# Head mixing for two groups at once on four 64x64 tiles of TensorE

## The chip, the core and the metric

The kernel runs on one core of a Trainium2 chip. The metric is the device time of one execution in microseconds. A core has a matrix engine (TensorE, PE in the profile, with PEld for its weight loads), a vector engine (VectorE, DVE), a scalar engine (ScalarE, ACT), a general engine (GpSimd, POOL) and a queue engine (SyncE, SP). The engines run side by side and wait for one another by semaphores; each works through its own instructions in the order in which the program issues them. TensorE writes to PSUM, a memory of eight banks, from which VectorE and ScalarE copy results to SBUF.

## The reference

Attention whose heads are mixed before and after the softmax, then a mixer over tokens and channels:

```python
batch, n_heads, seq, head_dim = (4, 12, 448, 64)

scores = scale * np.matmul(q, k.transpose(0, 1, 3, 2))
scores = np.einsum('bhij,hg->bgij', scores, w_pre)
scores = scores - np.max(scores, axis=-1, keepdims=True)
attn = np.exp(scores)
attn = attn / (np.sum(attn, axis=-1, keepdims=True) + 1e-09)
attn = np.einsum('bhij,hg->bgij', attn, w_post)
out = np.matmul(attn, v)          # [batch, head, seq, 64] -> x [batch, seq, 768]

xt = x.transpose(0, 2, 1)
h = np.maximum(xt @ w_tok1, 0.0) @ w_tok2      # 448 -> 256 -> 448
u = x + h.transpose(0, 2, 1)
h2 = np.maximum(u @ w_ch1, 0.0) @ w_ch2        # 768 -> 1536 -> 768
return u + h2
```

All of it is float32, and the head mixing (12x12) is what the change is about.

## The kernel before

**Row blocks and groups.** The 448 query rows of a batch are cut into four row blocks of 120, 120, 120 and 88 (`IT`); the 16 row blocks of all batches are numbered T. A row block is cut into *groups* of ten rows (`GR`), so it has 12 groups, or 9 in the last of a batch (eight of ten rows, one of eight). There are 180 groups in all, numbered G; `first[T]` is the first group of row block T. In a group, 10 rows x 12 heads = 120 pairs (row, head) lie on the partitions, with 448 key positions behind each. So one matmul with a 120x120 block matrix (`kpre`: `w_pre` repeated for each row) mixes the heads of ten rows.

**A group's way.** `qk` computes the scores of one head pair of a row block and evicts them from PSUM to the tile `s`, one head by ScalarE and one by VectorE; six such *score steps* make a row block. For T < 2 both heads sit in the two halves of the partitions and each matmul uses 64 rows of the array in float32; for T >= 2 queries are split into a rounded part and a remainder (type float32r), and a score step is four matmuls. `regroup` gathers a group's 120 rows by a DMA on the SP queue into a tile `r`. `pre` is the mixing matmul into a PSUM bank; `mx` takes the row maximum (VectorE); `ex` the exponential with its row sum (ScalarE); `rec` adds 1e-9, takes the reciprocal (VectorE) and scales the post-mixing matrix by it (GpSimd, tile `wr`). `post` is four matmuls with pieces of the exponential as stationary operand and `wr` as moving one, so it mixes heads, normalizes and transposes at once; `hi` (ScalarE) copies its PSUM bank to the tile `at`. After each two row blocks `end_av` issues a burst of `av` matmuls (attention times values, two heads on two column halves of the array), whose results go to DRAM. After the attention come the token mixer and the channel mixer, which the change does not touch.

**Splitting.** `conv_k` rounds one K head into a float32r tile and computes the remainder on GpSimd; `conv_q` does the same for half of a row block's queries. The rounding copy is VectorE's. `load_k`, `load_q` and `load_v` are their DMAs, on SP.

**Order of the work.** The order of issue is written out by hand. The main loop runs over G. In an iteration stand: `regroup` for groups ahead (up to 8 tiles `r`), loads that are due, `pre(G + 3)` (`AH = 3`), `rec(G + 2)`, `mx` and `ex` of G + 3, the score steps due (`qk_at`), an `av` burst at the start of every second row block, `post(G)`, `hi(G)`, and the splits due (`do`). The tables `qk_at` and `do` are filled before the loop: with `f = first[T - 1]`, the six score steps of row block T stand at groups f - 7 + h*n//6 with n = `first[T] - f - 3`; the splits of the next batch's K heads go two to a group.

PSUM has eight banks: two for `av`, two for `qk`, two for `pre`, two for `post`.

## Time and profile before

| | |
|---|---|
| time, median of 3 runs | 917.74 us (916.89 to 918.32) |
| the profiled execution | 916.27 us |
| its span, first to last instruction | 914.5 us |
| TensorE busy | 884.7 us |
| granted TensorE clock, mean | 0.998 |
| first and last `pre` start | 17.4 and 462.0 us |
| first and last `post` start | 22.8 and 467.3 us |
| first matmul of the channel mixer | 560.0 us |

The profile is one execution as the hardware recorded it. A row of its groups names the line of the kernel, the engine, the operation, output <- inputs, shapes and count, then the busy time in us and the mean ns of one, then the idle time of that engine just before these instructions with what ended it. A timeline row has start (us), length (us), engine, line, operation and count; consecutive instructions of a line are merged. A bracket at its end is the engine's idle time before it, with what ended it. A float32 matmul stands as two MATMUL records, a float32r matmul as one. Records of matmuls overlap, so the distance between starts, not the length, tells what one costs in a stream.

### The profile page before, as it was taken

How to read it: one execution, taken by the hardware profiler on the slowest of the kernel's cores; microseconds unless marked ns; L12 is line 12 of the kernel's file. 1: busy time of each engine (PE TensorE's matmuls, PEld its weight loads, DVE VectorE, ACT ScalarE, POOL GpSimd, SP SyncE). 2: the span in 40 equal slices, each digit the busy share in tenths (PEclk: the TensorE clock that was granted, in tenths of full speed). 3: DMA queues.
4: the chain of work that ended last, by engine and by line, in shares of the span. 5: the costliest groups of instructions: out<-in, count | busy, mean ns of one | idle time of the engine just before them, and what ended most of it. 6: DMA issues, size and time to landing. Idle time of an engine off the chain costs nothing.

```text
span 914.5 us, 14650 instructions
## 1 busy us (share of the span) xinstructions
PE 884.7 (97%) x5107; PEld 723.8 (79%) x5107; DVE 470.3 (51%) x1083; ACT 395.1 (43%) x941; POOL 321.8 (35%) x345
## 2 busy tenths in 40 slices
PE   8799899998999989999989999999999999999998
PEld 3467677776777767777767888999999999999997
DVE  3755664657646576463468999998310120031002
ACT  3366575665656557665675453443200100010000
POOL 1764743447434474341355567774000000000000
PEclk9999999999999999999999999999999999999999
DMA  5845445744457444542555666554400030000001
GB/s 167 196 144 153 113 137 134 200 144 119 137 141 193 146 118 137 142 151 94 128 188 157 202 231 192 174 165 146 177 0 1 1 121 1 1 27 34 0 1 61
DMA packets 75689, 109.16 MB, mean 119 GB/s; under 512 B 27729, under 2 KB 62048, under 8 KB 75104
## 3 DMA queue, kind: packets, MB, share of 16 engines
q1 hardware_dynamic: 68272, 101.64, 38.0%
q10 hardware_dynamic: 7312, 6.57, 2.3%
q8 instruction: 41, 0.67, 0.3%
q14 instruction: 32, 0.26, 0.1%
q0 software_dynamic: 32, 0.02, 0.0%
HBM read 53.15 MB, written 16.52 MB: 76 GB/s over the span
## 4 chain that ended last, share of the span: by engine, by line
PE 83%; DVE 6%; POOL 3%; issue 3%; ACT 2%; DMA 1%; SPq 1%; ACTq 0%; POOLq 0%; DVEq 0%
PE post L237 13%; PE pre L201 11%; PE av L254 7%; PE qk L181 7%; PE pc L514 6%; PE pc L515 6%; PE pc L513 6%; PE po L515 6%; PE po L514 6%; PE po L513 6%; PE pt L513 2%; PE pt L514 2%; PE pt L515 2%; ACT e L214 2%; DVE sm L207 2%
## 5 line engine op out<-in xcount | busy, mean ns | idle before, releaser
L237 PEld LDWEIGHTS post<-wr,e 120*112 120x112 f32 (+1 forms) x1440 | 172.7, 177 | 61.0 <-issue 36.4
L237 PE MATMUL post<-wr,e 120*112 120x120 f32 (+1 forms) x1440 | 179.8, 268 | 12.6 <-POOL wr L226 11.3
L201 PE MATMUL pre<-r,kpre 120*120 120x448 f32 x360 | 167.2, 547 | 5.0 <-ACT e L214 4.8
L214 ACT ACTIVATE e<-pre,sm 120x448 f32<-120x448 f32 x180 | 114.2, 634 | 129.8 <-DVE sm L207 129.2
L226 POOL TENSOR_SCALAR wr<-kpost,sm 120x120 f32<-120x120 f32 x180 | 110.4, 615 | 169.9 <-DVE sm L224 117.4
L207 DVE TENSOR_REDUCE sm<-pre 120x1 f32<-120x448 f32 x180 | 112.2, 623 | 103.2 <-PE pre L201 98.4
L510 DVE SCALAR_TENSOR_TENSOR rl<-pc,rh 128x448 fp32r<-128x448 f32 x48 | 29.9, 622 | 221.5 <-ACT rh L509 221.5
L509 ACT ACTIVATE rh<-pc 128x448 fp32r<-128x448 f32 x48 | 26.1, 543 | 238.2 <-PE pc L515 238.2
L181 PE MATMUL qk<-k,qc 128*120 128x448 f32 (+1 forms) x336 | 111.6, 453 | 0.2 <-ACT s L182 0.2
L514 PE MATMUL pc<-u,w 128*128 128x448 f32 x288 | 105.2, 365 | 0.0
L513 PE MATMUL pc<-u,w 128*128 128x448 f32 x288 | 105.2, 365 | 0.0
L515 PE MATMUL pc<-u,w 128*128 128x448 f32 x288 | 105.2, 365 | 0.0
L515 PE MATMUL po<-rh,w 128*128 128x448 f32 x288 | 105.2, 365 | 0.0
L513 PE MATMUL po<-rh,w 128*128 128x448 f32 x288 | 105.2, 365 | 0.0
L514 PE MATMUL po<-rl,w 128*128 128x448 f32 x288 | 105.2, 365 | 0.0
L243 ACT COPY at<-post 112x480 f32<-112x480 f32 x180 | 102.9, 571 | 5.2 <-PE post L237 5.0
L370 POOL TENSOR_SCALAR cv_g<-cv_g 128x384 f32<-128x384 f32 (+2 forms) x56 | 87.1, 1555 | 20.2 <-ACT cv_g L364 20.2
L181 PEld LDWEIGHTS qk<-k,qc 128*120 128x120 f32 (+1 forms) x336 | 58.2, 175 | 40.1 <-issue 26.9
L254 PE MATMUL av<-at,v 112*64 112x240 f32 (+1 forms) x768 | 74.6, 354 | 0.6 <-ACT x L265 0.6
L254 PEld LDWEIGHTS av<-at,v 112*64 112x64 f32 x768 | 54.4, 137 | 20.2 <-issue 1.5
L182 DVE COPY s<-qk 120x448 f32<-120x448 f32 (+1 forms) x96 | 59.7, 622 | 14.4 <-PE qk L176 8.2
L153 POOL TENSOR_TENSOR qc<-rq,qc 128x720 fp32r<-128x720 f32 (+1 forms) x28 | 46.6, 1663 | 40.7 <-DVE qc L152 32.1
(70 smaller groups left out, 1185.6 us busy)
## 6 DMA issues: line engine op xcount, KB each, us to landing
r<-s SPq DMA_DIRECT2D x176, 210.0 KB
cv_r<-in_w_ch_dram SPq DMA_DIRECT2D x48, 384.0 KB
rq<-in_q_dram SPq DMA_DIRECT2D x40, 180.0 KB
xr<-x_dr SPq DMA_DIRECT2D x8, 672.0 KB
u_dr<-u SPq DMA_DIRECT2D x24, 224.0 KB
ur<-u_dr SPq DMA_DIRECT2D x4, 1344.0 KB
out_dram<-ur SPq DMA_DIRECT2D x24, 224.0 KB
rk<-in_k_dram SPq DMA_DIRECT2D x18, 224.0 KB
```

The costliest lines, as they stand in the source:

```text
L181: nc.tensor.matmul(out=p[s][:n, :S], lhsT=l[:, g % 6, :], rhs=kt, start=i == 0, stop=i == 1)
L201: nc.tensor.matmul(out=p[:m, :S], lhsT=kpre[:m, :m], rhs=R.pop(G)[:m], start=True, stop=True)
L207: nc.vector.tensor_reduce(out=s[:m, 0:1], in_=PP[G][:m, :S], axis=AX.X, op=ALU.max, negate=True)
L214: nc.scalar.activation(out=e[:m], in_=PP.pop(G)[:m, :S], func=ACTF.Exp, bias=s[:m, 0:1], scale=1.0, accum_out=s[:m, 1:2])
L226: nc.gpsimd.tensor_scalar(out=w[:m, :m], in0=(kpost if n == GR else kpost8)[:m, :m], scalar1=s[:m, 3:4], scalar2=None, op0=ALU.mult)
L237: nc.tensor.matmul(out=p[:JP, j * m:(j + 1) * m], lhsT=l, rhs=w[:m, :m], start=True, stop=True)
L243: nc.scalar.copy(out=AT[:, :, :, o:o + IT[t][1]][:, :, :, rows(G)[1]], in_=PO.pop(G)[:JP, :JT * H * n].rearrange("p (j g i) -> p j g i", j ...
L254: nc.tensor.matmul(out=p[64 * s:64 * s + 64, :N], lhsT=V[:, 2 * hp + s, j, :], rhs=AT[:, j, 2 * hp + s, :N], start=j == 0, stop=j == JT - 1,)
L370: nc.gpsimd.tensor_scalar(out=g[:P], in0=g[:P], scalar1=MAG_MIN, scalar2=MAG_MAX, op0=ALU.max, op1=ALU.min,)
L513: nc.tensor.matmul(out=p, lhsT=a[0], rhs=x[0], start=first, stop=False)
L514: nc.tensor.matmul(out=p, lhsT=a[0], rhs=x[1], start=False, stop=False)
L515: nc.tensor.matmul(out=p, lhsT=a[1], rhs=x[0], start=False, stop=last)
```

## The change

Groups are worked on in pairs of neighbours (`steps`: pairs within a row block, the group of eight rows alone). The main loop runs over steps.

- `pre` for a pair: the 120 rows of each group's tile `r` now stand at partitions 4 to 123, so that five query rows lie in each half of 64 partitions. Four matmuls of 64 (or 60) rows by 64 columns use the four quarters of the array: array rows x take half x of both tiles, array columns s take group s. The bank of the pair's first group gets the first five query rows of both groups, the other bank the last five of both. `kpre` becomes one 60-column block in each half of the partitions; a group of eight rows uses its own matrix `kpre8` on the whole array.
- Tiles behind it have 128 partitions with four unused rows in each half; `kpost` has zeros there. `hi` writes two runs of five columns for each (key piece, head), where it wrote one of ten.
- `AH` is 2 steps (four groups). `pre` has four PSUM banks; `qk` uses the two banks of `av` (or two of `pre` in half of the first score steps).
- For T > 1 both score evictions are VectorE's. The rounding copies of `conv_k` and `conv_q` are ScalarE's.
- The splits of K heads go one to a group; the first row block's query split is two groups later, some K loads two or three groups earlier.
- At the start: three more small DMAs and ten memsets on GpSimd, and a few more operations for the constants.

The diff at its core:

```diff
-AH = 3
+AH = 2
...
-    kcat = mid.tile([120, 34], F32, bufs=1, name="kcat")
-    kpre = mid.tile([120, 120], F32, bufs=1, name="kpre")
-    kpost = mid.tile([120, 120], F32, bufs=1, name="kpost")
+    kcat = [mid.tile([128, 34], F32, bufs=1, name=f"kcat{i}") for i in range(2)]
+    kpre = mid.tile([128, 64], F32, bufs=1, name="kpre")
+    kpost = mid.tile([128, 120], F32, bufs=1, name="kpost")
+    kpre8 = mid.tile([96, 96], F32, bufs=1, name="kpre8")
     kpost8 = mid.tile([96, 96], F32, bufs=1, name="kpost8")
+    rt = [mid.tile([128, S], F32, bufs=1, name=f"r{i}") for i in range(NR)]
...
-        nc.vector.tensor_copy(out=t[p:p + 64], in_=r)
+        nc.scalar.copy(out=t[p:p + 64], in_=r)
...
-        nc.vector.tensor_copy(out=t[0], in_=r)
+        nc.scalar.copy(out=t[0], in_=r)
...
-            p = [ps.tile([128, 512], F32, tag=w, name="qk") for w in ("pre", "post")]
+            p = [ps.tile([128, 512], F32, tag="pre", bufs=4, name="qk") for s in range(2)]
         else:
-            p = [ps.tile([128, 512], F32, tag="qk", name="qk") for s in range(2)]
+            p = [ps_av.tile([128, 512], F32, tag="av", name="qk") for s in range(2)]
...
-            (nc.vector.tensor_copy if s else nc.scalar.copy)(out=S_t[T][:n, g, :], in_=p[s][:n, :S])
+            (nc.vector.tensor_copy if s or T > 1 else nc.scalar.copy)(out=S_t[T][:n, g, :], in_=p[s][:n, :S])
...
-        r = mid.tile([120, S], F32, tag="r", bufs=NR, name="r")
-        nc.sync.dma_start(out=r[:12 * n], in_=rows(G)[0](S_t[4 * b + t], 0))
-        R[G] = r
-
-    def pre(G):
-        m = 12 * groups[G][3]
-        p = ps.tile([128, 512], F32, tag="pre", name="pre")
-        nc.tensor.matmul(out=p[:m, :S], lhsT=kpre[:m, :m], rhs=R.pop(G)[:m], start=True, stop=True)
-        PP[G] = p
+        o = 4 if n == GR else 0
+        nc.sync.dma_start(out=rt[G % NR][o:o + 12 * n], in_=rows(G)(S_t[4 * b + t], 0))
+
+    def pre(st):
+        for g in st:
+            PP[g] = ps.tile([128, 512], F32, tag="pre", bufs=4, name="pre")
+        if len(st) == 1:
+            G = st[0]
+            nc.tensor.matmul(out=PP[G][:96, :S], lhsT=kpre8, rhs=rt[G % NR][:96], start=True, stop=True)
+            return
+        for x, g in enumerate(st):
+            k = slice(64 * x, 64 + 60 * x)
+            for s, a in enumerate(st):
+                nc.tensor.matmul(
+                    out=PP[g][64 * s:64 * s + 64, :S], lhsT=kpre[k], rhs=rt[a % NR][k], start=True, stop=True
+                )
+
+    def parts(G):
+        return 128 if groups[G][3] == GR else 96
...
-            out=w[:m, :m], in0=(kpost if n == GR else kpost8)[:m, :m], scalar1=s[:m, 3:4], scalar2=None, op0=ALU.mult
+            out=w[:m, :12 * n], in0=kpost if n == GR else kpost8, scalar1=s[:m, 3:4], scalar2=None, op0=ALU.mult
...
+            l = e[:k, JP * j:JP * j + JP]
+            nc.tensor.matmul(out=p[:JP, j * m:(j + 1) * m], lhsT=l, rhs=w[:k, :m], start=True, stop=True)
...
-        nc.scalar.copy(
-            out=AT[:, :, :, o:o + IT[t][1]][:, :, :, rows(G)[1]],
-            in_=PO.pop(G)[:JP, :JT * H * n].rearrange("p (j g i) -> p j g i", j=JT, g=H),
-        )
+        d = AT.rearrange("p j g i -> p (j g) i")
+        p = PO.pop(G)[:JP, :JT * H * n]
+        if n < GR:
+            d, p = d[:, :, o + 10:o + 88:11], p.rearrange("p (q i) -> p q i", i=n)
+        else:
+            w = 10 if t < 3 else 11
+            a = o + w * (c - c % 2)
+            d = d[:, :, a:a + 2 * w].rearrange("p q (s i) -> p q s i", s=2)[:, :, :, 5 * (c % 2):5 * (c % 2) + 5]
+            p = p.rearrange("p (q s i) -> p q s i", s=2, i=5)
+        nc.scalar.copy(out=d, in_=p)
...
-    nc.gpsimd.dma_start(out=kcat, in_=wcat)
+    for i in range(2):
+        nc.gpsimd.memset(kcat[i], 0.0)
+    nc.gpsimd.dma_start(out=kcat[0][4:124], in_=wcat)
+    for s in range(2):
+        nc.gpsimd.dma_start(out=kcat[1][64 * s:64 * s + 60], in_=wcat[60 * s:60 * s + 60])
+    nc.gpsimd.dma_start(out=kpre8[:, :34], in_=wcat[:96])
+    for r in rt:
+        nc.gpsimd.memset(r[:4], 0.0)
...
+    steps = []
+    G = 0
+    while G < NG:
+        n = 2 if groups[G][2] % 2 == 0 and groups[G][3] == GR else 1
+        steps.append(list(range(G, G + n)))
+        G += n
+    for st in steps[:AH]:
+        pre(st)
+        for g in st:
+            mx(g)
+            ex(g)
+    for g in steps[0]:
+        rec(g)
+    qk(1, 2)
+    pre_done = steps[AH][0]
...
-    for h in range(H):
-        at(h // 2, conv_k, 0, h)
+    for i, g in enumerate((0, 0, 1, 1, 2, 5, 6, 7, 8, 9, 9, 10)):
+        at(g, conv_k, 0, i)
     for T in range(2, NT):
         f = first[T - 1]
-        n = f if T == 1 else first[T] - f - 3
+        n = first[T] - f - 4
         for h in range(HP):
             g = f - LR + 3 + h * n // HP
             qk_at.setdefault(g, []).append((T, h))
             if T % 4 == 3 and T + 1 < NT:
-                c = [f - LR + 7 + max(0, 3 * i // 2) for i in (h, h - KB)]
-                at(c[1] + 2 if h >= KB else f - LR - 2 + h, load_k, T // 4 + 1, h)
-                for s in range(2):
-                    at(c[0] + s, conv_k, T // 4 + 1, 2 * h + s)
+                c = [f - 6 + i + 2 * (i > 6) for i in range(H)]
+                at(c[2 * (h - KB) + 1] + 1 if h >= KB else f - LR - 2 + h, load_k, T // 4 + 1, h)
+                for i in (2 * h, 2 * h + 1):
+                    at(c[i], conv_k, T // 4 + 1, i)
         if T > 2:
-            at(first[T - 2] - LR + 2, load_q, T)
+            at(first[T - 2] - LR + 2 + (T == 3), load_q, T)
         for hf in range(2):
-            at(f - LR - 1 + hf, conv_q, T, hf)
-
-    for G in range(NG):
-        b, t, c, n = groups[G]
-        burst = c == 0 and t % 2 == 0 and G > 0
-        ahead = G + AH < NG
-        if (b, t, c) == (B - 1, 3, 1):
-            close("early")
-            open_prep()
-            cv_tick(2)
-            load_x(0)
-        while done_r < min(NG, G + LR + 1) and len(R) < NR:
+            at(f - LR - 1 + hf + 2 * (T == 2), conv_q, T, hf)
...
+    for i, st in enumerate(steps):
+        while done_r < min(NG, st[0] + LR + 2, pre_done + NR):
             regroup(done_r)
             done_r += 1
-        for fn, *a in do.get(G, []):
-            if fn in (load_k, load_q):
-                fn(*a)
-        if t == 0 and b and 1 <= c < 5:
-            load_v(b, c - 1)
-        if ahead:
-            pre(G + AH)
-        if G + AH - 1 < NG:
-            rec(G + AH - 1)
-        if ahead:
-            mx(G + AH)
-            ex(G + AH)
-        for a in qk_at.get(G, []):
-            qk(*a)
-        if burst:
-            end_av(*groups[G - 1][:2])
-        post(G)
-        hi(G)
-        for fn, *a in do.get(G, []):
-            if fn in (conv_k, conv_q):
-                fn(*a)
-        if (b, t) == (B - 1, 3) and c:
-            cv_tick(c % 2)
-            if c == 5:
-                load_x(1)
+        nxt = steps[i + AH] if i + AH < len(steps) else []
+        for G in st:
+            b, t, c, n = groups[G]
+            if (b, t, c) == (B - 1, 3, 1):
+                close("early")
+                open_prep()
+                cv_tick(2)
+                load_x(0)
+            for fn, *a in do.get(G, []):
+                if fn in (load_k, load_q):
+                    fn(*a)
+            if t == 0 and b and 1 <= c < 5:
+                load_v(b, c - 1)
+            if G == st[0]:
+                if nxt:
+                    pre(nxt)
+                    pre_done += len(nxt)
+                for g in steps[i + 1] if i + 1 < len(steps) else []:
+                    rec(g)
+                for g in nxt:
+                    mx(g)
+                    ex(g)
+            for a in qk_at.get(G, []):
+                qk(*a)
+            if c == 0 and t % 2 == 0 and G > 0:
+                end_av(*groups[G - 1][:2])
+            post(G)
+            hi(G)
+            for fn, *a in do.get(G, []):
+                if fn in (conv_k, conv_q):
+                    fn(*a)
+            if (b, t) == (B - 1, 3) and c:
+                cv_tick(c % 2)
+                if c == 5:
+                    load_x(1)
     close("ps", "mid")
     a2 = en("a2", bufs=2, side="right")
```

More of the change, by code (lines that the diff above doesn't have):

```diff
@@ L210, in ex @@
     def ex(G):
-        m = 12 * groups[G][3]
-        e = mid.tile([120, S], F32, tag="e", bufs=6, name="e")
+        m = parts(G)
+        e = mid.tile([128, S], F32, tag="e", bufs=6, name="e")
         s = SM[G]
@@ L219, in rec @@
     def rec(G):
-        n = groups[G][3]
-        m = 12 * n
+        m, n = parts(G), groups[G][3]
         s = SM.pop(G)
@@ L224, in rec @@
         nc.vector.reciprocal(out=s[:m, 3:4], in_=s[:m, 2:3])
[L225 removed]
+        w = mid.tile([128, 120], F32, tag="wr", bufs=4, name="wr")
         nc.gpsimd.tensor_scalar(
[L227 removed]
+            out=w[:m, :12 * n], in0=kpost if n == GR else kpost8, scalar1=s[:m, 3:4], scalar2=None, op0=ALU.mult
         )
@@ L231, in post @@
     def post(G):
-        m = 12 * groups[G][3]
+        k, m = parts(G), 12 * groups[G][3]
         p = ps.tile([128, 512], F32, tag="post", name="post")
@@ L235, in post @@
         for j in range(JT):
-            l = e[:m, JP * j:JP * j + JP]
-            nc.tensor.matmul(out=p[:JP, j * m:(j + 1) * m], lhsT=l, rhs=w[:m, :m], start=True, stop=True)
+            l = e[:k, JP * j:JP * j + JP]
+            nc.tensor.matmul(out=p[:JP, j * m:(j + 1) * m], lhsT=l, rhs=w[:k, :m], start=True, stop=True)
         PO[G] = p
@@ L301, in attn_mixer_kernel @@
         qk(1, h)
-    for G in range(AH):
-        pre(G)
-        mx(G)
-        ex(G)
-        if G:
-            rec(G - 1)
-        if G == 1:
-            qk(1, 2)
+    steps = []
[13 more added lines that the diff above has]
+    pre_done = steps[AH][0]
     done_r = NR
```

44 lines of the change are left out of this document (28 added, 16 removed).

## The prediction

> **What bounds the kernel now.** I read the busy line first, then the chain of work that ended last, then the windows by stage, the groups by line, and last the timeline of one engine. The first three say where the limit lies.
>
> ```profile
> PE 884.7 (97%) x5107; PEld 723.8 (79%) x5107; DVE 470.3 (51%) x1083; ACT 395.1 (43%) x941; POOL 321.8 (35%) x345
> ...
> PE 83%; DVE 6%; POOL 3%; issue 3%; ACT 2%; DMA 1%; SPq 1%; ACTq 0%; POOLq 0%; DVEq 0%
> ...
> 60.00:460.00 400.00, 391.19 (x2617) 293.31 (x2616) 230.00 (x627) 251.05 (x627) 182.42 (x226) 1.00 0.51 143
> ```
>
> The columns of the window row are PE, PEld, DVE, ACT, POOL, clock, DMA share, GB/s. TensorE is busy 391 of 400 us in the attention stage at full granted clock; the others have 37 to 54% to spare. The channel and token mixing after it is untouched by the diff, so the answer must come from the attention stage.
>
> Steady state of that stage, TensorE alone (start, length):
>
> ```profile
> 54.11 0.98 PE L237 MATMUL post<-wr,e 120*112 120x120 f32 x8
> 54.93 0.92 PE L201 MATMUL pre<-r,kpre 120*120 120x448 f32 x2
> 55.68 0.98 PE L237 MATMUL post<-wr,e 120*112 120x120 f32 x8
> ...
> 58.06 0.98 PE L237 MATMUL post<-wr,e 120*112 120x120 f32 x8
> ...
> 60.45 0.98 PE L237 MATMUL post<-wr,e 120*112 120x120 f32 x8
> ```
>
> A group costs 0.82 us of `post` (54.11 to 54.93) and 0.75 us of `pre` (to 55.68), 1.57 us in all; with one score step (`qk`, four matmuls) it is 2.39 us (58.06 to 60.45), so a score step is 0.82. Starts, not lengths, are the price, because matmuls overlap. A float32 matmul stands as two records, here called passes, of about 0.37 us for 448 columns. The groups whose durations I use (busy, mean ns of one, idle before):
>
> ```profile
> L237 PE MATMUL post<-wr,e 120*112 120x120 f32 x1408 | 176.2, 268 | 12.6 <-POOL wr L226 11.3 <-ACT at L243 1.3
> L214 ACT ACTIVATE e<-pre,sm 120x448 f32<-120x448 f32 x176 | 111.7, 635 | 127.5 <-DVE sm L207 127.0
> L207 DVE TENSOR_REDUCE sm<-pre 120x1 f32<-120x448 f32 x176 | 109.7, 624 | 103.2 <-PE pre L201 98.4 <-POOL wr L226 3.0 <-PE qk L181 0.7
> L226 POOL TENSOR_SCALAR wr<-kpost,sm 120x120 f32<-120x120 f32 x176 | 108.2, 616 | 166.4 <-DVE sm L224 114.0 <-PE qk L181 40.7 <-PE pre L201 4.9
> L243 ACT COPY at<-post 112x480 f32<-112x480 f32 x176 | 99.4, 565 | 5.2 <-PE post L237 5.0
> L182 DVE COPY s<-qk 120x448 f32<-120x448 f32 x72 | 44.9, 623 | 12.9 <-PE qk L176 8.2 <-PE qk L181 0.6
> L126 POOL TENSOR_TENSOR k<-rk,k 64x448 fp32r<-64x448 f32 x36 | 41.4, 1158 | 33.1 <-DVE k L125 27.1 <-issue 4.2
> L254 PE MATMUL av<-at,v 112*64 112x240 f32 x384 | 39.8, 367 | 0.0
> L182 ACT COPY s<-qk 120x448 f32<-120x448 f32 x72 | 37.7, 523 | 8.3 <-PE qk L176 8.3
> L153 POOL TENSOR_TENSOR qc<-rq,qc 128x720 fp32r<-128x720 f32 x20 | 36.0, 1802 | 37.7 <-DVE qc L152 29.1 <-DVE sm L223 8.0
> L125 DVE CAST k<-rk 64x448 fp32r<-64x448 f32 x36 | 26.9, 765 | 0.0
> L152 DVE CAST qc<-rq 128x720 fp32r<-128x720 f32 x20 | 16.6, 832 | 4.4 <-DMA rq<-in_q_dram 4.4
> L243 ACT COPY at<-post 112x384 f32<-112x384 f32 x4 | 3.4, 858 | 0.0
> L274 POOL DMA_DIRECT2D kcat<-in_wcat_dram x1 | 0.8, 757 | 0.8 <-POOLq L662 0.8
> ```
>
> **Step 1: `pre` on four tiles.** Of 180 groups 176 form 88 pairs (18 in each batch's first three row blocks, 4 in the last) and 4 stay single. A pair costs 1.50 us now. The new pair is four matmuls, each of half the rows and half the columns, two passes each. The trace has both halves of the idea, not the whole. Column halves: `av` issues 384 records of 240 columns in 39.8 us, 0.104 each; by the 0.373 for 448 columns one alone would take 0.20, so two run at once. Row halves: the first score steps (L176) use them.
>
> ```profile
> 19.25 1.02 PE L176 MATMUL qk<-kraw,q 64*120 64x448 f32 x4
> 20.20 1.76 PE L201 MATMUL pre<-r,kpre 120*120 120x448 f32 x4
> 21.89 1.02 PE L176 MATMUL qk<-kraw,q 64*120 64x448 f32 x4
> 22.84 1.07 PE L237 MATMUL post<-wr,e 120*112 120x120 f32 x8
> 23.75 0.54 PE L201 MATMUL pre<-r,kpre 120*120 120x448 f32 x1
> ```
>
> Four L176 records, two tiles by two passes, end after 1.02 us; one after another their four starts alone would spread over 1.1. So both tiles' first passes run together, then both second passes. But the visit has edges: 21.89 to 22.84 is 0.95, which is 0.20 over two passes; the `post` behind it takes 0.91 and not 0.82; and the two `pre` before it take 1.69 and not 1.50, 0.19 for leaving the visit before (19.25) and entering this one, so about 0.10 for the entry. A visit costs 0.95 + 0.09 + 0.10 = 1.14 us. I take 1.14 for four tiles: 0.36 below 1.50. Bounds: 0.75 (no edges) and 4 x 0.373 + 0.39 = 1.88 (two tiles at a time).
>
> The Trainium skill bears on this place. "TensorE: Matmul & The Clock Gate", Part 3, says that matmuls start and end strictly in program order. The program order here is first pass, second pass, next tile; a tile's second pass can't join its first, so four tiles would take five passes in a staircase. By that rule a visit is 5 x 0.373 + 0.39 = 2.26 us, and the row above speaks against it, since the two-tile staircase would need three passes, 2 x 0.373 + 0.54 = 1.28 us, where the row has 1.02.
>
> **Step 2: both score evictions of row blocks 2 to 15 on VectorE, in the two `av` banks.** `qk` loses its own two banks (the four `pre` banks take them), which are otherwise free between `av` bursts. ScalarE loses 84 copies of 0.52; VectorE gains 84 of 0.62. The order on VectorE in one iteration is four small operations (about 0.6 in all), two maxima, then the evictions; what queues behind the maxima are these evictions, and the second score step waits for them. I place a pair with two score steps by hand, zero at the start of its `pre` visit, consecutive VectorE operations 0.57 apart (they overlap a little): second passes start at 0.57, the maxima run at 1.15 and 1.72, the first step's evictions at 2.28 and 2.85. TensorE: first score step 1.04 to 1.90, `post` to 2.72; the second step's first bank is free at 2.95 and its second at 3.52, so it ends at 3.90 where 3.54 was due, and the second `post` ends at 4.72 to 4.75. Now it is 2 x 2.39 = 4.78. So such a pair gains nothing: the 0.36 of step 1 is eaten by the eviction queue. With one score step or none the whole 0.36 stays. The schedule (h*n//6 with n = 8, or 5 behind a short block) puts two score steps into 31 pairs, one into 19 and three into single groups, none into 38. 57 x 0.36 = 20.5 us.
>
> "TensorEngine Tiling (Array Packing)", Performance Considerations, in the Trainium skill warns of just this: tiling speeds up TensorE but not PSUM evacuation, and both ScalarE and VectorE should evict. Taken literally for every pair it leaves nothing of the 20.5 us.
>
> **Step 3: rounding copies on ScalarE, and splitting spread.** Now two K heads are rounded in each of six groups, and VectorE and GpSimd take turns on them. It stalls TensorE in batches 0 to 2 and at the start:
>
> ```profile
> 212.34 0.98 PE L237 MATMUL post<-wr,e 120*112 120x120 f32 x8
> 216.10 1.07 PE L237 MATMUL post<-wr,e 120*112 120x120 f32 x8 [1.41 <-POOL wr L226]
> 219.85 1.07 PE L237 MATMUL post<-wr,e 120*112 120x120 f32 x8 [1.12 <-POOL wr L226]
> ...
> 213.14 2.20 POOL L153 TENSOR_TENSOR qc<-rq,qc 128x720 fp32r<-128x720 f32 x1
> ...
> 216.31 3.03 DVE L125 CAST k<-rk 64x448 fp32r<-64x448 f32 x2
> ...
> 33.42 0.54 DVE L152 CAST qc<-rq 128x720 fp32r<-128x720 f32 x1 [4.43 <-DMA rq<-in_q_dram]
> 42.41 1.07 PE L237 MATMUL post<-wr,e 120*112 120x120 f32 x8 [1.00 <-POOL wr L226]
> ```
>
> 212.34 to 216.10 is 3.76 where 1.57 was due, the next 3.75 (one score step) where 2.39 was due: 3.55 us lost, three times over the batches, 10.7. The weights `wr` come late because the splits sit before them on GpSimd, and the casts ahead of the maxima on VectorE grow to 1.5 us each. After: one head per group, so GpSimd has at most 2 x 0.62 + 2 x 1.16 = 3.6 us in a pair, or 4.2 with a query split (1.80) in the place of one head's; only pairs without scores (2.78) are shorter, `wr` is asked for one pair later, and the pair at 24 has an `av` burst (96 x 0.104 = 10 us) in it. ScalarE per pair: 2 x (0.63 + 0.50) plus at most 0.84 + 0.52 for copies (its 0.52 for 448 columns, scaled), 3.6 us, over 2.78 only in the pair at 26. I take 8 of 10.7 us. At the start: from 22.84 to 60.45 twelve groups, six score steps and three L176 steps (1.14) should take 18.8 + 4.9 + 3.4 = 27.1 us and take 37.6. The query copy waits there on VectorE for its DMA until 33.4, with maxima behind it; it moves two groups later and to ScalarE, where it would hold back the exponentials and `hi` copies instead, for less long, as the queue has advanced. I place `post` 5 at about 37, not 42.4, and block 1 two more us ahead: 7 us of 10.5. Bounds of both: nothing, and 21.
>
> Moved DMAs: the K loads of the last two head pairs go out two to three groups earlier, each behind the split that frees its buffer; what waits behind them on SP are gathers for eight groups ahead. Nothing. Three more POOL DMAs (0.76 each), ten memsets and the wider constants precede the first `wr`, for which GpSimd idles 14 us; VectorE's constants now wait for the fourth of these DMAs, but its first eviction comes at 9.5 us anyway:
>
> ```profile
> 20.43 0.59 POOL L226 TENSOR_SCALAR wr<-kpost,sm 120x120 f32<-120x120 f32 x1 [14.17 <-DVE sm L224]
> 9.51 1.38 DVE L182 COPY s<-qk 120x448 f32<-120x448 f32 x2 [3.48 <-PE qk L176]
> ```
>
> Nothing; without that cover 3 us.
>
> **Step 4: the dependency loop.** Where no score step stretches a group the loop exponential, sum, reciprocal, maximum, exponential is longer than TensorE's 1.57:
>
> ```profile
> 450.29 0.63 ACT L214 ACTIVATE e<-pre,sm 120x448 f32<-120x448 f32 x1 [0.57 <-DVE sm L207]
> ...
> 451.05 0.15 DVE L223 TENSOR_SCALAR sm<-sm 120x1 f32<-120x1 f32 x1 [0.85 <-ACT e L214]
> ...
> 451.32 0.62 DVE L207 TENSOR_REDUCE sm<-pre 120x1 f32<-120x448 f32 x1
> 452.04 0.63 ACT L214 ACTIVATE e<-pre,sm 120x448 f32<-120x448 f32 x1 [0.57 <-DVE sm L207]
> ```
>
> 450.29 to 452.04 is 1.75. In the last block about ten groups run at it: 10 x 0.18 = 2 us. By pairs the loop is 1.75 + 0.63 = 2.4, under 2.78, so it goes.
>
> **Step 5: `hi` in runs of 5 instead of 10.** Nothing on the path: ScalarE frees the first `post` bank about 0.2 us before it is wanted. The cost is between 0.565 and the 0.858 of the single-element form (384 elements); at runs half as long I take 0.60. At 0.86 ScalarE would need 3.0 in pairs of 2.78: 5 to 8 us.
>
> **Sum.** 20.5 + 8 + 7 + 2 = 37.5 us. The profiled execution took 916.27 (span 914.5, 1.8 around it), 1.5 below the median 917.74. 916.3 - 37.5 = 878.8 for it, 880 on the scale of the median.
>
> **Rivals.**
> (a) Two tiles at a time, the other side. Each visit 1.88: 57 pairs lose 0.38 and 31 lose 0.73 (all their evictions start later), 44 us, against 17 from steps 3 and 4: 945. It turns slower when a visit exceeds 1.57 us. For it: no row shows four tiles. Against: row pairs and column pairs both overlap fully. Chance 0.06.
> (b) The staircase, visit 2.26: 88 x 0.76 = 67, and 31 x 0.4 in the eviction queue, less 17: about 980. Chance 0.03. It is what the page's strict order would make.
> (c) Evictions don't hold up the second score step and visits lose an edge: 31 x 0.36 = 11 more and some 4, 865. For it: the placing by hand has margins of 0.2 us. Against: VectorE holds 4.0 us of work in 4.4. Chance 0.15.
> (d) ScalarE takes over the stalls: its queue holds exponentials behind copies that wait for a DMA or the splits, steps 3 and 4 give 2 and not 17: 895, with dearer `hi` copies 902. Chance 0.13.
> (e) The gains of step 1 and the losses of step 2 cancel (evictions queue over into one-step pairs) and (d) holds too: within 0.2%. Chance 0.03.
>
> **Numbers.** The forecast, 868 to 893, has 0.60. The range 858 to 903 takes in (c) and (d). This kernel's runs spread by 0.15%, so 0.2% is about what can be told from no change. Faster 0.88, same 0.03, slower 0.09.
>
> **What would show it.** Four `pre` records start within some 0.03 us, the next four 0.47 later, and 1.14 us lie from visit start to unchanged pace; a pair of groups takes 2.78 without scores, 3.6 with one step, 4.75 with two, where second score matmuls wait for VectorE; `post` waits for `wr` no more than 3 us in all; L126 no longer waits for VectorE; post of group 12 starts near 52 us; `hi` about 0.60. A visit over 1.5 us, or pairs bound by ScalarE, would make the prediction wrong.

## The result, and the profile after

The changed kernel took 892.99 us (median of four runs, 889.94 to 893.65) beside 917.83 for the kernel before in the same session: ratio 0.9724, 95% interval 0.9701 to 0.9748. That is 24.8 us, where I had said 37.5. The time stands at the upper edge of the forecast (868 to 893) and nearer to rival (d)'s 895 than to the sum's 880, so the number alone proves little; the traces below have to tell which account holds. The profiled execution took 892.98 us with a span of 891.2.

One thing must be known to read times below: in the channel mixer, which no kernel here changes, matmuls came 202.7 ns apart in some executions and 206.7 ns in others, 6.8 us over that stage (last section); the profiles of the first four experiments have the slower pace. So experiments are compared by stretches of their profiles: from the first `post` of group 12 (G12) to the last `post`, on to the first matmul of the token mixer, and on to the end. Three profiles whose attention is the same took 377.66, 377.69 and 378.05 us from G12 to the last `post`, so a difference of under 0.4 us there says little.

The page of the profile after: busy line, chain, the window of steady state, groups.

```profile
PE 859.5 (96%) x5459; PEld 687.5 (77%) x5459; DVE 458.4 (51%) x1096; ACT 400.7 (45%) x933; POOL 316.3 (35%) x358
PE 74%; issue 10%; DVE 6%; ACT 4%; DMA 3%; POOL 3%; ACTq 0%; POOLq 0%; DVEq 0%; SPq 0%
60.00:440.00 380.00, 371.22 (x2983) 262.96 (x2984) 227.87 (x659) 256.61 (x621) 179.49 (x233) 1.00 0.55 154
L248 PE MATMUL post<-wr,e 128*112 128x120 f32 (+1 forms) x1440 | 176.5, 270 | 4.9 <-POOL wr L237 2.5
L263 ACT COPY at<-post 112x480 f32<-112x480 f32 x180 | 110.0, 622 | 42.8 <-PE post L248 42.3
L209 PE MATMUL pre<-r,kpre 64*64 64x448 f32 (+1 forms) x704 | 89.9, 566 | 4.5 <-DMA r<-s 4.5
```

TensorE still bounds the attention. `post` waits 2.5 us for `wr`, where it waited 11.3 before; a new wait, 4.5 us for a gather, stands at `pre`. The timeline of TensorE through three kinds of pair, and two rows of VectorE in the last of them:

```profile
148.03 0.98 PE L209 MATMUL pre<-r,kpre 64*64 64x448 f32 x8
148.94 1.89 PE L248 MATMUL post<-wr,e 128*112 128x120 f32 x16
150.77 0.98 PE L209 MATMUL pre<-r,kpre 64*64 64x448 f32 x8
...
154.50 0.98 PE L209 MATMUL pre<-r,kpre 64*64 64x448 f32 x8
155.41 1.07 PE L183 MATMUL qk<-k,qc 128*120 128x448 f32 x4
...
157.35 1.20 PE L183 MATMUL qk<-k,qc 128*120 128x448 f32 x4
...
159.31 0.98 PE L209 MATMUL pre<-r,kpre 64*64 64x448 f32 x8
...
156.68 1.15 DVE L184 COPY s<-qk 120x448 f32<-120x448 f32 x2
158.06 1.16 DVE L184 COPY s<-qk 120x448 f32<-120x448 f32 x2 [0.23 <-PE qk L183]
```

Without a score step a pair takes 2.74 us (148.03 to 150.77), with one 3.73 or 3.55 (150.77 to 154.50; 3.55 where nothing is late), with two 4.81. In the last, the second score step starts at 157.35, after the copies of 156.68 have freed its first bank.

Where the time went, before to after: G12 starts at 60.45 and 62.55 (2.1 lost); from there to the last `post` 406.83 and 377.66 (29.2 gained); to the token mixer 13.82 and 16.30 (2.5 lost); to the end 433.39 and 434.69 (1.3 lost). Together 23.3 of span.

The 2.1 before G12 is less firm than the rest. In six profiles of this same start (the changed kernel twice, and four edits that act later) G12 stands at 59.81 to 64.85 us, on the whole the later the more windows of 3.41 us in which the granted clock was 0.50 (half clock, from here on) lie before it: 59.81 and 60.01 with one, 62.03 and 62.55 with two, 62.48 with three, 64.85 with four. The profile before has one such window, so beside its like (60.45 to 59.81 and 60.01) the start lost nothing. And at G12 the changed kernel has issued `pre` for 18 groups where the kernel before had issued it for 16: a visit of 1.1 us has only changed sides.

### The profile page after: what moved, and what is told of

It is laid out like the page before. It is cut to its first block, busy times and chain, and to the rows that moved or that the text cites. A ratio compares the mean times of both kernels' runs of the same rounds, so it can differ in the third digit from the quotient of the medians.

```text
span 891.2 us, 15218 instructions
## 1 busy us (share of the span) xinstructions
PE 859.5 (96%) x5459; PEld 687.5 (77%) x5459; DVE 458.4 (51%) x1096; ACT 400.7 (45%) x933; POOL 316.3 (35%) x358
## 4 chain that ended last, share of the span: by engine, by line
PE 74%; issue 10%; DVE 6%; ACT 4%; DMA 3%; POOL 3%; ACTq 0%; POOLq 0%; DVEq 0%; SPq 0%
PE post L248 8%; PE pc L560 7%; PE pc L559 7%; PE pc L561 7%; PE po L560 6%; PE po L559 6%; PE po L561 6%; PE qk L183 6%; PE pre L209 6%; PE av L271 4%; DVE sm L219 3%; PE pt L559 2%; DVE s L184 2%; PE pt L560 2%; PE pt L561 2%
## 5 line engine op out<-in xcount | busy, mean ns | idle before, releaser
L248 PEld LDWEIGHTS post<-wr,e 128*112 128x112 f32 (+1 forms) x1440 | 163.7, 177 | 50.8 <-POOL wr L237 21.8
L248 PE MATMUL post<-wr,e 128*112 128x120 f32 (+1 forms) x1440 | 176.5, 270 | 4.9 <-POOL wr L237 2.5
L219 DVE TENSOR_REDUCE sm<-pre 128x1 f32<-128x448 f32 x180 | 104.2, 620 | 120.2 <-PE pre L209 118.8
L237 POOL TENSOR_SCALAR wr<-kpost,sm 128x120 f32<-128x120 f32 x180 | 103.0, 584 | 112.7 <-DVE sm L234 72.1
L226 ACT ACTIVATE e<-pre,sm 128x448 f32<-128x448 f32 x180 | 112.7, 632 | 61.3 <-DVE sm L219 61.0
L263 ACT COPY at<-post 112x480 f32<-112x480 f32 x180 | 110.0, 622 | 42.8 <-PE post L248 42.3
L184 DVE COPY s<-qk 120x448 f32<-120x448 f32 (+1 forms) x180 | 104.6, 618 | 25.1 <-PE qk L183 17.9
L183 PE MATMUL qk<-k,qc 128*120 128x448 f32 (+1 forms) x336 | 94.2, 397 | 6.3 <-POOL k L128 3.4
L209 PE MATMUL pre<-r,kpre 64*64 64x448 f32 (+1 forms) x704 | 89.9, 566 | 4.5 <-DMA r<-s 4.5
L414 POOL TENSOR_SCALAR cv_g<-cv_g 128x384 f32<-128x384 f32 (+2 forms) x56 | 86.4, 1543 | 20.6 <-ACT cv_g L408 20.5
L183 PEld LDWEIGHTS qk<-k,qc 128*120 128x120 f32 (+1 forms) x336 | 50.0, 174 | 46.5 <-DVE sm L235 17.1
```

Source lines behind the costliest of these rows:

```text
L183: nc.tensor.matmul(out=p[s][:n, :S], lhsT=l[:, g % 6, :], rhs=kt, start=i == 0, stop=i == 1)
L184: (nc.vector.tensor_copy if s or T > 1 else nc.scalar.copy)(out=S_t[T][:n, g, :], in_=p[s][:n, :S])
L209: nc.tensor.matmul(out=PP[g][64 * s:64 * s + 64, :S], lhsT=kpre[k], rhs=rt[a % NR][k], start=True, stop=True)
L219: nc.vector.tensor_reduce(out=s[:m, 0:1], in_=PP[G][:m, :S], axis=AX.X, op=ALU.max, negate=True)
L226: nc.scalar.activation(out=e[:m], in_=PP.pop(G)[:m, :S], func=ACTF.Exp, bias=s[:m, 0:1], scale=1.0, accum_out=s[:m, 1:2])
L237: nc.gpsimd.tensor_scalar(out=w[:m, :12 * n], in0=kpost if n == GR else kpost8, scalar1=s[:m, 3:4], scalar2=None, op0=ALU.mult)
```

## Experiments

Each is an edit of the changed kernel. They ran in three sets of four, each on a chip of its own, with the kernel before beside them (923.09, 918.48 and 919.02 us).

**The tiles alone taken back.** `pre` is one 124x128 matmul for each group again (and `hi` writes runs of ten).

```diff
-        for x, g in enumerate(st):
-            k = slice(64 * x, 64 + 60 * x)
-            for s, a in enumerate(st):
-                nc.tensor.matmul(out=PP[g][64 * s:64 * s + 64, :S], lhsT=kpre[k], rhs=rt[a % NR][k], ...)
+        for g in st:
+            nc.tensor.matmul(out=PP[g][:, :S], lhsT=kpre[:124], rhs=rt[g % NR][:124], start=True, stop=True)
```

> The changed kernel with the four quarter-array matmuls of a pair replaced by one whole-array matmul per group (124 rows by 128 columns); pairs, banks, copies, schedule as changed; `hi` in runs of ten again. Theory: a visit of four tiles costs 1.10 us (pair without scores 911 + 1825 ns, less 2 x 0.82) against 1.50, so the 57 pairs with no or one score step lose 0.41 each, 23.4 us; the 31 pairs with two lose nothing, as the eviction queue sets them (4.81 now, 4.77 by the same placing by hand). 893 + 22 = 915, within 2 us of the kernel before. Rival (the tiles bring little, the gain is the splits and the loop): under 900.

914.43 us (ratio to before 0.991, interval 0.9884 to 0.9936). The 915 expected was met in part by luck: 6.8 us of the profiled execution are the slower pace of the channel mixer, and the tiles cost less than the 23.4 of the expectation. Its pairs, by the timeline:

```profile
150.54 1.68 PE L207 MATMUL pre<-r,kpre 124*128 124x448 f32 x4
152.05 1.80 PE L244 MATMUL post<-wr,e 128*112 128x120 f32 x16
153.69 1.68 PE L207 MATMUL pre<-r,kpre 124*128 124x448 f32 x4
```

3.15 us a pair against 2.74. G12 to the last `post` takes 395.00 us, 17.3 more than with tiles. The other 11.9 of the 29.2 come from the rest of the change. By row block (start of its first `post` to that of the next block) the tiles are worth 1.7, 1.5 and 1.1 to 1.3 us in the first, second and third of a batch, 2.25 in the very last third one, and almost nothing in the fourth: 27.87 us without them, 27.84 with them.

**One score eviction back on ScalarE**, for every row block.

```diff
-            (nc.vector.tensor_copy if s or T > 1 else nc.scalar.copy)(out=S_t[T]...
+            (nc.vector.tensor_copy if s else nc.scalar.copy)(out=S_t[T]...
```

> The changed kernel with the score evictions of row blocks 2 to 15 shared again, one head on ScalarE and one on VectorE. Theory: the second score step of a pair waits for VectorE's eviction queue; with two evictions less there it starts on time, a pair with two steps takes 4.4 instead of 4.81 us, 31 x 0.38 = 12 us less: 881. Rival 1: ScalarE's queue, with 2 x 0.52 more behind its exponentials, holds up `hi` and `post` instead: 890 to 900. Rival 2 (the two-step pairs are set by something else, the `wr` of GpSimd or the visit): within 2 us of 893.

909.44 us (0.9875, 0.9823 to 0.9927), and 388.51 from G12 to the last `post`: 10.9 worse, a clear miss, and G12 itself stands at 66.93. A two-step pair takes 5.01 to 5.05 us, not less than 4.81. ScalarE's timeline shows why:

```profile
164.19 0.63 ACT L226 ACTIVATE e<-pre,sm 128x448 f32<-128x448 f32 x1 [0.78 <-DVE sm L219]
164.72 0.19 ACT L226 ACTIVATION_READ_ACCUMULATOR e<-pre,sm 128x1 f32 x1
164.81 0.63 ACT L226 ACTIVATE e<-pre,sm 128x448 f32<-128x448 f32 x1
165.33 0.20 ACT L226 ACTIVATION_READ_ACCUMULATOR e<-pre,sm 128x1 f32 x1
165.43 0.53 ACT L184 COPY s<-qk 120x448 f32<-120x448 f32 x1
```

The pair's first score step ran from 163.33. VectorE took its half at 164.60; ScalarE takes the other only after both exponentials, and the second step's matmuls into that bank start at 166.01, when the copy of 165.43 is done. An engine with free time is no help where its queue comes late.

**Score steps spread, one to a pair**, in all row blocks from the fourth on, with the query splits moved to match.

```diff
+            if T > 2:
+                g = f + (-10, -9, -8, -6, -4, -3)[h] if T % 4 == 0 else f - 9 + 2 * h
...
-            at(f - LR - 1 + hf + 2 * (T == 2), conv_q, T, hf)
+            at(f - LR + 1 + hf if T == 2 else f - 12 + 3 * hf, conv_q, T, hf)
```

> The changed kernel with the score steps of row blocks 3 to 15 spread one to a pair (groups f - 9 + 2h; in front of each batch's first block f - 10, -9, -8, -6, -4, -3), query splits at f - 12 and f - 9; the number of score steps stays. Pairs with two steps go from 31 to 8. Theory: a pair with two steps (4.81) and one without (2.74) become two with one (2 x 3.55), 0.44 less each, 23 x 0.44 = 10 us, and no two query splits fall in one pair, which now costs about 0.9 in each of three batches: 893 - 12 = 881. Rival (two-step pairs aren't dearer for being two-step): 890 to 893. A scores tile is reused two groups earlier than now; if its gathers haven't landed, VectorE waits and it is slower.

895.58 us (0.9718, 0.967 to 0.9766), a miss as a total; 376.29 from G12 to the last `post`, 1.4 better. The first row block of a batch got shorter, 21.29 for 22.37 us, and the last 24.6 for 27.83; but a query split directly ahead of its use, behind a key split, cost it again in the third (25.83 for 23.52; TensorE, then GpSimd), and two of the second row blocks got longer too (33.70 and 33.30 for 32.30):

```profile
204.74 0.87 PE L183 MATMUL qk<-k,qc 128*120 128x448 f32 x3 [1.31 <-POOL qc L155]
...
201.71 1.14 POOL L128 TENSOR_TENSOR k<-rk,k 64x448 fp32r<-64x448 f32 x1 [10.82 <-issue]
202.93 1.76 POOL L155 TENSOR_TENSOR qc<-rq,qc 128x720 fp32r<-128x720 f32 x1
```

**The start reordered.** The values are loaded after the first gathers, the constants for groups of eight stand behind the first scores.

```diff
-    for part in range(JT):
-        load_v(0, part)
...
+            if G in (6, 7, 8, 9):
+                load_v(0, G - 6)
```

> The changed kernel with two things moved at the start: the value loads of batch 0 (1.3 MB, eight DMAs on SP) go from behind the first eight gathers to groups 6 to 9, and VectorE's and GpSimd's constants for the groups of eight rows go behind the first score steps. Theory: the fifth pair's `pre` waits 4.1 us and then 1.7 more for gathers that SP issues behind these loads and the query loads; with 1.3 MB less in front (about 8 us at the 170 GB/s of this stretch) the wait goes, and the first eviction starts 0.8 earlier: 5 us less, 888. Rival (the query loads alone set it, or the score step behind them): 892 to 893.

898.78 us (0.973, 0.9667 to 0.9794); G12 at 60.98, 1.6 earlier and not 5, which lies within the spread of the unchanged start. What the trace shows is that the gathers no longer hold up the fifth pair, and that the score step behind it then waits 2.0 us for the query split:

```profile
34.93 0.98 PE L209 MATMUL pre<-r,kpre 64*64 64x448 f32 x8
...
39.96 0.88 PE L183 MATMUL qk<-k,qc 128*120 128x448 f32 x3 [2.02 <-POOL qc L155]
```

**The changed kernel again, and the end of attention.** In the second kernel the weight-splitting step behind the fifth of the last six output products stands behind the sixth.

```diff
-            if (b, t) == (B - 1, 3):
-                cv_tick(1)
+            if (b, t) == (B - 1, 3) and hp != HP - 2:
+                cv_tick(1 + (hp == HP - 1))
```

> The changed kernel itself, unchanged, so that the others of this set have a base on the same chip. Expected 890 to 894 us as in its first profile (892.98). What is looked at is the granted clock: if the half-clock stretch in the start (8.42 to 11.84 us in the first profile) belongs to the chance time at which the first keys land, it moves or goes; if the one after attention (455.57 to 462.39) belongs to the wait of the token stage for the last copy of attention's output, it comes again at the same place, with the first matmul of the token stage about 2.5 us late.

> The weight-splitting step that stood behind the fifth of the last six output products moves behind the sixth, so that ScalarE copies the last product out before it rounds and takes magnitudes. Theory A (the token stage is late because the last copy stands behind weight splitting in ScalarE's queue, and the half-clock stretch follows from TensorE's idle time): the 2.47 us wait shrinks to 1 us or less, the half-clock stretch goes (6.83 us at half clock hold back about half of that), together about -4 us against the unchanged kernel: 887 to 889. Rival B (what is moved comes back in the token stage, where the weights are wanted): within 1 us of the unchanged kernel, with a new wait for the split weights in the first token products.

The unchanged one: 893.73 us (0.9718, 0.9664 to 0.9773). Its half-clock stretch behind attention came again (452.89 to 459.72) after the same wait. The one in the start did too (9.16 to 12.57), but not in the run of the edit, whose start is the same: TensorE's wait for the first keys was 1.80 us in the one and 1.15 in the other. The other: median 897.43 us (0.9703, 0.9645 to 0.9761; 886.29 to 900.28), so the total shows no gain; what follows is read from the profiled executions, 888.99 us against 890.35 of the unchanged. The wait for the copy fell from 2.5 to 0.8 us, the half-clock stretch is gone, and last `av` to the end of the span took 433.8 us, where the unchanged kernel needs 437.6: the 3.8 that theory A had put at 4. The first window row is the changed kernel's in its first profile, the second that of the edit; the clock is the number behind the five engines, 0.66 and 1.00:

```profile
454.00:464.00 10.00, 7.53 (x25) 6.29 (x24) 6.53 (x13) 3.46 (x10) 7.21 (x8) 0.66 0.64 188
```

```profile
452.00:462.00 10.00, 9.08 (x52) 7.21 (x53) 7.83 (x15) 5.39 (x17) 9.22 (x10) 1.00 0.79 227
```

**The rounding copies back on VectorE.**

```diff
-        nc.scalar.copy(out=t[p:p + 64], in_=r)     # conv_k; conv_q likewise
+        nc.vector.tensor_copy(out=t[p:p + 64], in_=r)
```

> The rounding copies of keys and queries go back to VectorE; the two-at-a-time mixing stays. Theory A (the mid-batch stall of before came from GpSimd's subtractions running against VectorE's copies, and ScalarE removed it): the long interval in the middle of each batch comes back, 2.6 us in three batches, about +8 us, and more at the start: about 900. Rival B (VectorE, with the two-score pairs still its burden, pays for the copies in those pairs as well): each of the 31 pairs with two score steps gets longer than 4.81 us, +12 or more: 905. Rival C (the copies are hidden): 893.

891.13 us (0.9671, 0.963 to 0.9712); G12 to the last `post` 377.14 against 377.69. Rival C. The 0.5 is a balance: each of three last row blocks got 0.7 shorter (27.14 for 27.84), second and third ones up to 0.65 longer. This one overthrew my reason for the gain in mid-batch, and led to the next pair.

**The old places of the key splits**, first with ScalarE's copies, then with VectorE's and the old start as well.

```diff
-                c = [f - 6 + i + 2 * (i > 6) for i in range(H)]
+                c = [f - LR + 7 + max(0, 3 * i // 2) for i in (h, h - KB)]
...
-                for i in (2 * h, 2 * h + 1):
-                    at(c[i], conv_k, T // 4 + 1, i)
+                for s in range(2):
+                    at(c[0] + s, conv_k, T // 4 + 1, 2 * h + s)
```

> The splits of the next batch's keys go back to the old places, two heads in some groups and some beside a query split; their rounding copies stay on ScalarE. Putting these copies back on VectorE alone had changed almost nothing (891.13 us). Theory A (what took the mid-batch stall away is the placing, which leaves the two groups of the query split without a key split): the row blocks in which these splits stand get 2 to 3.5 us longer, in three batches, 6 to 10 us more by the time of the last post. Rival B (either of the two, placing or engine, is enough): under 1 us a batch here, and the stall only comes back when both are undone.

> The whole split part undone: old places of the key splits, start included, the query split of the first row blocks two groups earlier, rounding copies on VectorE; tiles and evictions stay as changed. Theory A (placing alone): as with the old places and ScalarE's copies, within 1 us a batch, third row block of a batch 2 to 3.5 us longer than in the changed kernel. Rival B (either is enough): only this one shows the 3.55 us stall per batch. The start tells what that part was worth there: if my 7 us existed and something else ate them, post of group 12 is at 67 to 70 us; if the part brought nothing there, at 60 to 64.

902.73 us (0.9825, 0.9785 to 0.9864) and 899.96 (0.9797, 0.9762 to 0.9833). From G12 to the last `post` 387.80 and 385.25 against 377.69: placing is worth 10.1 us with ScalarE's copies (387.80), and 8.1 with VectorE's (385.25 against the 377.14 of the run above). Theory A: of the 10.1, 9.7 stand in the three third row blocks where these splits stand (26.69, 27.03 and 26.84 us for 23.51 to 23.87). The same place in four kernels, first the changed one, then VectorE's copies, old places, and both:

```profile
206.75 1.07 PE L248 MATMUL post<-wr,e 128*112 128x120 f32 x8 [0.33 <-POOL wr L237]
```

```profile
211.05 1.20 PE L183 MATMUL qk<-k,qc 128*120 128x448 f32 x4 [1.01 <-DVE s L184]
```

```profile
209.58 1.44 PE L248 MATMUL post<-wr,e 128*112 128x120 f32 x8 [2.50 <-POOL wr L237]
...
203.84 3.33 POOL L128 TENSOR_TENSOR k<-rk,k 64x448 fp32r<-64x448 f32 x3 [9.04 <-issue]
207.24 1.73 POOL L155 TENSOR_TENSOR qc<-rq,qc 128x720 fp32r<-128x720 f32 x1
208.96 1.13 POOL L237 TENSOR_SCALAR wr<-kpost,sm 128x120 f32<-128x120 f32 x2
```

```profile
215.12 1.54 PE L183 MATMUL qk<-k,qc 128*120 128x448 f32 x4 [2.33 <-DVE s L184]
```

With the old places, three key splits and a query split, 5.1 us, stand ahead of `wr` in GpSimd's queue. Which engine rounds only decides who shows the wait. Not all of the loss is waiting. With ScalarE's copies TensorE's waits for `wr` from 60 us on grow by 6.7 us (2.5 to 9.2); and in both kernels each of the three stalls is followed by a window at half clock, here that of the stall just shown:

```profile
206.73:210.14 3.41, 0.91 (x9) 0.56 (x6) 1.48 (x5) 3.41 (x9) 3.28 (x4) 1.00 0.39 85
210.14:213.55 3.41, 3.41 (x13) 2.42 (x12) 1.25 (x2) 2.27 (x7) 3.22 (x3) 0.50 0.37 108
```

The changed kernel and the kernel before have no such window at these stalls. The start of the last kernel: G12 at 64.39, within what the changed start itself gives (59.81 to 64.85), so the new splitting brought nothing there that can be told.

**The second half of one query split moved by a group.**

```diff
-            at(f - LR - 1 + hf + 2 * (T == 2), conv_q, T, hf)
+            at(f - LR - 1 + hf + 2 * (T == 2) + hf * (T % 4 == 1), conv_q, T, hf)
```

> One edit on the changed kernel: the second half of the query split that stood in the same pair as the first, at the end of each third row block, moves one group on. If the two 3.4 us of GpSimd subtractions in one pair cause the wait of post for its weights at the start of the last row block, intervals of 1.19 and 3.46 us there become 0.82 and 2.74 plus the pair's steps, 0.8 to 1.0 us in each of three batches, last post 2.5 to 3 us earlier against the post of group 12; if not, nothing.

891.41 us (0.9707, 0.9672 to 0.9743). The first three intervals between starts of `post` in the last row block sum to 6.06 us, in the changed kernel to 6.37 (1.19, 3.46, 1.72): a third of what I expected, 0.3 a batch. With VectorE's copies they sum to 5.68. In the run with all steps spread the first two are 0.82 and 2.74, without a wait; which of its two moves, of score steps or of query splits, did that no run tells.

**The repairs together**, and then with the third row block of a batch spread too: first score steps one to a pair except at the end of the second (and third) row block; the constants, loads and weight splits as in the two runs above on start and end, key and query splits of the start in another order; the query splits for the next batch's first row block (T % 4 == 0) earlier, so that they lie under a burst of `av`.

```diff
+            if T % 4 in (1, 2):
+                g = (5, 7, 8, 9, 11, 13)[h] if T == 2 else f - 9 + 2 * h
+            elif T % 4 == 3:
+                g = f - (9, 7, 5, 3, 2, 1)[h]
+            else:                                      # second version only
+                g = f - (11, 9, 7, 5, 4, 3)[h]
...
-            at(f - LR - 1 + hf + 2 * (T == 2), conv_q, T, hf)
+            at(1 + 2 * hf if T == 2 else f - 13 + 2 * hf if T % 4 == 0 else f - 12 + 3 * hf, conv_q, T, hf)
```

> A version that puts the repairs together: score steps one to a pair in the first and last tile of a batch, the two halves of a query split in different pairs, the order of the first key and query splits, the values loaded after the first gathers, the eight-row constants behind the first scores, five more warm-up products, and the weight split behind the last output product. By the intervals seen in the earlier runs: first tile of a batch -1.1 in three batches, second -0.5 in four, last -2.5 in three, start -3, end of attention -4, in all about -20: 873. If the moved score steps bring new waits for query splits or late gathers as in the run with all steps spread (895.58 us), 885 to 890; if the work only moves within the batch, 887.

> The combined version of before (872.62 us) with the score steps of a batch's third row block spread from its second group on, their query split two groups earlier so that its GpSimd part lies under the burst of output products, and one of the first score steps a group later. Two-score pairs there fall from three to one, each 1.26 us over two single ones, and the 0.4 and 0.6 us waits in that block go: about -1.5 in each of three batches, -1 at the start: 867. If the early query split delays the weights of the groups behind the burst, or the gathers come late, 873 to 876.

In the first version `qk` of T = 2 has 6 and 7 for 7 and 8, and the query split of T % 4 == 0 stays. 872.62 us (0.9484, 0.944 to 0.9528) and 867.11 (0.9448, 0.9409 to 0.9487), both totals as expected, and well under both kernels. The terms of the first were not all met, so that its total is partly luck: first row blocks -1.05 (-1.1 expected) and the start -4.8 (-3), but the last ones -3.3 (-2.5), the second +0.2, once +1.6 (-0.5), and the third +0.7, for which nothing stood. In the second version the third ones got 1.5 shorter, as expected. Busy line and TensorE's waits from G12 to the last `post` of the second:

```profile
PE 845.8 (98%) x5464; PEld 685.2 (79%) x5464; DVE 454.3 (53%) x1096; ACT 401.7 (46%) x933; POOL 317.1 (37%) x358
```

```profile
PE post L248 <- ACT at L263: 1.3, 3, 0.7
PE av L271 <- ACT at L263: 0.8, 3, 0.3
PE qk L183 <- DVE s L184: 0.5, 1, 0.5
```

Against the changed kernel in the second session: G12 at 52.15 for 59.81, G12 to the last `post` 364.75 for 377.69, on to the token mixer 13.57 for 16.31, to the end 433.60 for 434.75. This profile has no half-clock window at all, where that of the changed kernel has three ahead of its last 5 us. All of it comes from moving work in time, and from the clock that this holds up; the operations are the same, but for five more warm-up products.

## Why the prediction was right, and where not

The sign, the bound and the size of the attention's gain were right; by the profiles 23.3 us came of 37.5; of the 14.2 that are missing, 9.1 went before G12, where I had put 7 of gain and 2.1 were lost in this pair of profiles, 3.8 after attention, where I had put nothing, and 1.3 between. That the 1.3 is so small is partly luck, since the tiles gave less than their term and the rest more (below). And the spread of 0.15% that I took from three runs was too small: beside the experiments the kernel before took 915.8 to 927.2 us, 1.2%.

*Step 1, right.* A pair without scores takes 2.74 us (I said 2.78), one with a score step 3.55 (3.6); 2.74 less two `post` of 0.82 is 1.10 for a visit (1.14). All eight passes of one visit start within half a microsecond, weights included:

```profile
L209 PEld LDWEIGHTS pre<-r,kpre x8: 129/130/133, 420.6 to 420.7; 64*64 64x64 f32 x4, 60*64 60x64 f32 x4
L209 PE MATMUL pre<-r,kpre x8: 536/562/587, 420.6 to 421.1; 64*64 64x448 f32 x4, 60*64 60x448 f32 x4
```

Rivals (a) and (b) fell with this. The first passes of all four tiles started 7 ns apart, the second passes 0.43 us behind them, so there is no staircase. The strict order of "TensorE: Matmul & The Clock Gate", Part 3, in the Trainium skill is one of whole matmuls; the four starts, in program order, agree with it, and the staircase was my own reading of it for two passes. I had 20.5 us for the term, 19.1 of it (53 of the 57 pairs) after G12; taking the tiles back costs 17.3 there. What is missing lies in the last row blocks. In three of them two halves of a query split fell into one pair and nothing was gained (27.83 us against 27.77 before); moving one half away gave back 0.3 us a batch. I had looked at such pairs for GpSimd's sum, not for its order.

*Step 2, right.* Two-step pairs gain nothing (4.81 us against 4.77 before, I said 4.75), for the reason given. The remedy of "TensorEngine Tiling (Array Packing)", Performance Considerations, in the Trainium skill, to evict with both engines, was not one here: 5.05 us with ScalarE taking half. Spreading the steps was.

*Step 3, mid-batch: size right, cause half wrong.* I credited ScalarE's rounding and the spreading with 8 us together. The whole split part is worth 7.6 (385.25 less 377.69), the placing of the key splits 8 to 10, ScalarE's rounding -0.5.

*Step 3, the start: failed.* I placed `post` 5 at 37 and G12 near 52 us, from a cast on VectorE that waited for its query load. The cast left VectorE, but three other things stood behind it (SyncE, VectorE, TensorE):

```profile
23.01 6.76 SPq L163 DMA_DIRECT2D v<-in_v_dram  x7
29.81 2.90 SPq L147 DMA_DIRECT2D rq<-in_q_dram  x4
32.82 7.02 SPq L197 DMA_DIRECT2D r<-s  x8
...
9.77 0.18 DVE L320 COPY k<-kpre 96x34 f32<-96x34 f32 x1 [3.56 <-DMA kpre<-in_wcat_dram]
...
38.77 2.67 PE L209 MATMUL pre<-r,kpre 64*64 64x448 f32 x8 [4.12 <-DMA r<-s]
```

The gathers from group 8 on are issued at 32.82, behind loads of values and queries, and `pre` waits 4.1 us for one of them; `post` 5 came at 43.66 (40.5 to 44.4 in the six profiles of this start, so 37 was missed by all). The score steps behind wait for the query split (2.0 us in the reordered start) and for the key splits (3.4 us up to G12 in the changed kernel). And the constants that I had put at nothing, with 3 us if their cover went, lost that cover: the first eviction starts at 10.62, right behind them, not at 9.51. Only with all of these moved did G12 come to 55.01 and 52.15, the first with one half-clock window before it and the second with none. So about 7 us were there to be had, but not by this change.

*After attention, "untouched": failed.* The token mixer's first product waits for ScalarE's copy of the last output product, which stands behind a rounding of weights that itself waited for VectorE (ScalarE, then TensorE; before, that product followed `av` at once, at 481.10):

```profile
455.22 0.38 ACT L423 CAST t<-cv_a 128x224 fp32r<-128x224 f32 x1 [1.35 <-DVE cv_a L442]
455.50 0.54 ACT L408 ACTIVATE cv_g<-cv_r 128x384 f32<-128x384 f32 x1
455.95 0.51 ACT L282 COPY x<-av 128x120 f32<-128x120 f32 x2
...
456.51 0.69 PE L559 MATMUL pt<-xn,t 128*128 128x384 f32 x1 [2.47 <-ACT x L282]
```

That is 2.5 us of waiting; the stage behind it took 1.3 longer, with 6.8 us of it at half clock. The run with the splitting step moved gave all of these 3.8 back: 447.1 us from the last `post` to the end, before 447.2.

*Steps 4 and 5.* Tiles 17.3 and the split part 7.6 leave 4.3 of the 29.2. About 1.5 of this is the two more groups whose `pre` stands ahead of G12 in the untiled run. The loop shows in that run's last two row blocks, which hold no score step and no key split: 19.62 and 12.87 us before (to the start of the last `post`), 19.01 and 9.64 there, 3.8 less; without the 1.5 I estimate 2.3 for the loop and the end of the stage, where I had 2. The last 0.5 stays open. `hi` takes 622 ns and not 600, off the path. Rival (c) was not seen, and of (d) only the 0.7 us that ScalarE's rounding costs in each of three last row blocks.

## What to carry to other kernels

A stage that gets shorter meets the queues around it at another phase: before the gain is booked, place each load, split and copy in its own engine's order at the stage's beginning and end, where no steady state covers it. Where a stall names an engine, test place and engine apart: here the order in GpSimd's queue was worth 8 to 10 us and the choice of the engine that rounds half a us, the other way. And once a critical engine has less to do, spread what remains one piece to a period; rearranging alone gave another 26 us here.

## What the hardware showed that I had not expected

- The granted clock goes by windows of 3.41 us. In the 14 profiles, where TensorE had been idle for 2.0 us or more of a window at full clock, the next was at half clock each time; up to 1.5 us it never was; between these both occurred. (Idle time is counted between the records, whose ends are modelled.) Two short waits add up. The page "TensorE: Matmul & The Clock Gate", Part 1, in the Trainium skill names a whole idle window of about 3.4 us; here 2.0 us in one were always enough.
- The channel mixer has two paces at the same granted clock. Two windows of 100 us, the first of the changed kernel in the second session, the second of the first combined version; the first count is matmuls:

```profile
600.00:700.00 100.00, 100.00 (x495) 92.69 (x494) 23.98 (x44) 13.87 (x27) 4.57 (x3) 1.00 0.16 59
```

```profile
600.00:700.00 100.00, 100.00 (x486) 90.82 (x485) 21.46 (x37) 12.78 (x25) 0.00 (x0) 1.00 0.15 55
```

Over the whole stage, 1728 matmuls, it is 350.07 and 356.90 us, or 202.7 and 206.7 ns from start to start. All four profiles on the first chip had the slower pace, one of the eight on the other two, and neither of the profiles of before and after. The attention's intervals do not show it (2.74 us a pair in both). I did not find its cause.
